# A spectral filter beside an MLP on one core: two-tile width transforms over four PSUM banks, PSUM in zones, leftover rows gathered, the filter chain with fillers in pieces

## The chip, the core and the metric

One core of a Trainium2 chip. TensorE (PE) multiplies matrices from SBUF into PSUM (eight banks), VectorE (DVE), ScalarE (ACT) and GpSimd (POOL) work element by element, SyncE (SP) issues all transfers of this kernel. [...] The metric is the device time of one execution in microseconds (us): 191.66 is the median of three runs of the kernel before (191.43 to 191.84).

## The reference

The input is one sequence of 2048 rows of 640, in bf16. It is normalised by rows, and the output is the input plus two branches of the normalised rows: a filter in the two-dimensional Fourier domain, and an MLP with a GELU.

```python
xn = _layernorm(x, axis=-1)                      # x: (1, 2048, 640)
X  = rfft2(xn.astype(float32)) * (w_r + 1j*w_i)  # w: (2048, 321)
a  = irfft2(X, s=(2048, 640)).astype(bfloat16)
h  = gelu(xn @ w1 + b1)                          # w1: (640, 1536)
return x + a + (h @ w2 + b2)                     # w2: (1536, 640)
```

## The kernel before

The 2048 rows lie on the 128 partitions as 16 tiles of 128 rows by 640 columns. The Fourier transforms are matmuls with constant tables, and a length-2048 transform is split into 128 x 16. The program runs through these steps; the names are those that the rows of the profile show.

1. *Ring*, for each of the 16 tiles `c`: DVE takes the statistics of `XV` (two halves, `stats`), aggregates them (`mv`), adds epsilon (`ve`); POOL raises it to the power -1/2 (`rstd`, one operation for two tiles, L538); DVE makes the shift (`nmr`) and the normalised tile (`T`, L553). PE transposes it with five matmuls against `ident` (L560) into one PSUM bank `tps`, and DVE or ACT copies that to `xnT`, the MLP's operand. DVE also folds the tile about its middle, twice (L572 and L575, into `T` again): 640 columns become four groups of 160. The first transform along the rows, `aps`, multiplies the folded tile by `gtab`: of each group 128 columns as a full matmul, and the 32 left over as a narrow one, 32 columns of output wide, four of them side by side on the partitions of one bank. A copy brings it to `XW` (DVE or ACT).
2. *MLP, first half*: 48 products `hps` of five 128 x 512 matmuls each (`ps<-xnT,W`), each followed by ACT's GELU into `gT` (L598). They need only four finished tiles of `xnT`, so they serve as filler wherever PE would wait.
3. *Filter chain*, for each of 8 pairs of row frequencies. `bps`: the width transform with `etab`, in two halves `v`, each over two banks, both members `n` of the pair beside each other in a bank; per half and member, 128 rows and the 32 left over are multiplied apart (the function `five`). Copies to `Xb`. `cps`: the second part of the row transform with `mtab`, 64 x 64 matmuls, in two halves `r`; copies to `Y`. On DVE the complex product with the filter weights `Wf`: two `T` of 1288 elements (L650), then two `Z` of 644 (L655). `dps`: back with `ntab`, in two halves `hi`, each 8 full matmuls and 8 narrow ones for the leftover 32 rows; copies to `XV`, of which the first use is over.
4. *End*, for each of 8 pairs of tiles: `eps`, the width transform back with `getab` (the same `five`), copies to `Wf` (whose weights are used up), two unfoldings on DVE (L700 and L705), then for each tile `fps`: 24 matmuls of the MLP's second half (`ps<-XW,gT`, with `W2` loaded over `XW`) and 2 with `htab` that add the last part of the row transform. POOL has meanwhile added the bias to the tile of `x` that was loaded once more (`xo<-xr,b2bc`, L713); DVE adds this to `fps` (`ost`, L725), and SP stores it.

The order is not written by hand. The kernel records its operations with their readers, writers, priorities and an estimated duration for each engine that may do it, and a small list scheduler (`Sched.schedule`) walks through simulated time: at each engine it takes, of the operations that could start within 0.03 us of the first, the one of highest priority. PSUM banks and SBUF buffers come out of pools in the same walk (`Pool.find`). `gate` keeps an operation back until others are placed. The result is one fixed list for each engine, in which every instruction waits for its semaphores in order. What is late on the chip is not overtaken: an engine waits at the head of its list. All DMAs are issued by SP, in the order of the program.

Of the kernel before, what the change touches and what calls it, by code (L numbers as in the profile page):

```python
# [13 lines left out]
D = 640  # L14
# [98 lines left out]

class Buf:


    def __init__(self, name, pool=None, size=1):
        self.name, self.pool, self.size = name, pool, size
        self.writers, self.readers = [], []
        self.slot = None  # L120
        self.prev = []
        self.left = None


class Pool:
# [8 lines left out]
    def find(self, size):  # L134
        best = None
        for i in range(0, len(self.free) - size + 1, size):
            if any(self.busy[i:i + size]):
                continue
            t = max(self.free[i:i + size])
            if size == 1 and len(self.free) == 8:  # L140
                t += 0.001 * (not self.busy[i ^ 1])
            if best is None or t < best[0]:
                best = (t, i)
        return best
# [17 lines left out]

LAT = {"pe": 0.2, "dve": 0.12, "act": 0.15, "pool": 0.1}


class Sched:
    def __init__(self, nc, engines):
# [5 lines left out]
    def op(self, engs, prio, emit, reads=(), writes=(), after=(), nbytes=0, gate=()):  # L173
        o = Op()
        o.gate = [g for g in gate if g is not None]
        o.name = writes[0].name if writes else ""
        o.engs = engs
        o.eng = None
        o.prio = prio
        o.emit = emit  # L180
        o.reads, o.writes, o.after = list(reads), list(writes), list(after)
        o.nbytes = nbytes
        o.seq = len(self.ops)
        o.done = False
        o.inc = False
        o.count = None
        o.sem = None
# [8 lines left out]
    def schedule(self):  # L196
# [15 lines left out]
        def avail(o):  # L212
            o.ready = max([0.0] + [d.end for d in o.deps])
# [6 lines left out]
        while left:  # L220
            best = None
            for e in self.engines:
                cands = []
                for o in pend[e]:
# [3 lines left out]
                    ok = True  # L228
                    for b in o.writes:
                        if b.pool is not None and b.slot is None:  # L230
                            f = b.pool.find(b.size)
# [3 lines left out]
                            r = max(r, f[0])  # L235
                    t = max(r, free[e])
                    if ok and len(o.engs) > 1:
                        mine = (t + dict(o.engs)[e], self.engines.index(e))
                        ok = all(e2 == e or (max(r, free[e2]) + d2, self.engines.index(e2)) > mine for e2, d2 in o.engs)
# [27 lines left out]
            for b in o.writes:  # L267
                if b.pool is not None and b.slot is None:
                    b.pool.take(b, b.pool.find(b.size)[1])
# [102 lines left out]
def bass_parallel_sum__spectral_gfnet__dense_activation_gelu__prompt_kernel(  # L372
# [21 lines left out]
    with ExitStack() as es:  # L394
# [32 lines left out]
        Zb = sb("Z", [128, 2, 4 * KP])  # L427
        ost = sb("ost", [128, 3, D])
# [17 lines left out]
        p_xn, p_x1, p_xf, p_xb, p_y, p_t, p_z = Pool(4), Pool(3), Pool(4), Pool(2), Pool(2), Pool(2), Pool(2)  # L446
        p_yo, p_y2, p_yf, p_xr, p_xo, p_os = Pool(3), Pool(2), Pool(3), Pool(4), Pool(3), Pool(3)

        def load(dst, src, buf, nbytes, after=(), reads=()):
            return K.op([("sp", 0.06)], 0, lambda e, _: e.dma_start(dst, src), reads=reads, writes=[buf], after=after, nbytes=nbytes)  # L450
# [8 lines left out]
        def copy(dst, src):  # L459
            def f(e, name):  # L460
                if name == "act":
                    return e.activation(dst(), src(), ACT.Copy)  # L462
# [12 lines left out]
        B_x = [Buf(f"x{g}") for g in range(4)]  # L475
# [4 lines left out]
        def load_x(g):  # L480
            load(view(XV, 4 * g * D, [[1, 4 * D]]), xv[:, 4 * g:4 * g + 4, :].rearrange("p c d -> p (c d)"), B_x[g], 4 * D * 256)
        load_x(0)
        load(ident[:], const["I"], B_id, 32768)
        for j in range(3):
            load(W1[:, :, 512 * j:512 * j + 512], w1v[:, :, 512 * j:512 * j + 512], B_w1s[j], 655360)
            if j == 0:
                load(b1t[:], b1v, B_b1, 3072)
# [273 lines left out]
```

## Time and profile before

| | |
|---|---|
| median of 3 runs | 191.66 us |
| the profiled execution | 190.8 us |
| its span, first to last instruction | 189.2 us |
| PE busy | 163.8 us (87%), 1505 matmuls |
| DVE, ACT, POOL busy | 99.7, 84.5, 28.5 us |
| mean granted clock of TensorE | 0.97 |

The profile is of one execution. Its page gives for each engine the busy share of 40 equal slices of the span in tenths, and the groups of instructions with count and duration; the trace behind it answers with the chain of waits that ended last, timelines of an engine, and sums by window. A timeline's row has the start, the length from the first start to the last end, the engine, the line, the names (`out<-in`) and the count; in brackets stands the idle time before it and what ended that. The names leave out buffer numbers: `ps` is any PSUM bank, `W` is `W1`, `XW` is `XW2`, which later holds `W2`, and `T` holds several of the ring's buffers. `L455` and `L462`/`L463` are helpers that issue all matmuls and all copies, so rows are told apart by their names. Matmuls are pipelined: the busy column of two neighbours overlaps.

### The profile page before, as it was taken

How to read it: one execution, taken by the hardware profiler on the slowest of the kernel's cores; microseconds unless marked ns; L12 is line 12 of the kernel's file. 1: busy time of each engine (PE TensorE's matmuls, PEld its weight loads, DVE VectorE, ACT ScalarE, POOL GpSimd, SP SyncE). 2: the span in 40 equal slices, each digit the busy share in tenths (PEclk: the TensorE clock that was granted, in tenths of full speed). 3: DMA queues.
4: the chain of work that ended last, by engine and by line, in shares of the span. 5: the costliest groups of instructions: out<-in, count | busy, mean ns of one | idle time of the engine just before them, and what ended most of it. 6: DMA issues, size and time to landing. Idle time of an engine off the chain costs nothing.

```text
span 189.2 us, 3594 instructions
## 1 busy us (share of the span) xinstructions
PE 163.8 (87%) x1505; PEld 99.7 (53%) x1505; DVE 99.7 (53%) x248; ACT 84.5 (45%) x123; POOL 28.5 (15%) x32
## 2 busy tenths in 40 slices
PE   0039999996049999999999999999999999998992
PEld 0035555552035454665656576766766676445771
DVE  0998899993055539889191853353524352000311
ACT  2018767755016499999968802020223021661000
POOL 1110111100631000000000013222241225000200
PEclk9999999999658999999999999999999999999998
DMA  6999999999320000000940003232222201000021
GB/s 176 378 388 275 98 110 99 106 96 287 101 83 0 3 0 0 7 3 0 280 139 3 0 13 95 69 107 69 69 71 71 69 35 52 21 0 0 35 69 38
DMA packets 14279, 16.64 MB, mean 88 GB/s; under 512 B 1208, under 2 KB 13496, under 8 KB 14264
## 3 DMA queue, kind: packets, MB, share of 16 engines
q1 hardware_dynamic: 14264, 16.42, 38.9%
q8 instruction: 12, 0.20, 0.5%
q14 instruction: 3, 0.02, 0.1%
HBM read 13.79 MB, written 2.62 MB: 87 GB/s over the span
## 4 chain that ended last, share of the span: by engine, by line
PE 67%; SPq 14%; DMA 10%; DVE 3%; POOL 3%; ACT 1%; issue 1%
PE ps L455 66%; SPq L450 14%; DMA xr<-in_A_x_dram 7%; DMA XV<-in_A_x_dram 2%; POOL xo L713 2%; DVE stats L534 1%; PE ps L560 1%; DVE Y L463 1%; POOL rstd L538 1%; DVE ost L725 0%; ACT XV L462 0%; ACT gT L598 0%; ACT Y L462 0%; DVE T L553 0%; DVE mv L536 0%
## 5 line engine op out<-in xcount | busy, mean ns | idle before, releaser
L455 PE MATMUL ps<-xnT,W 128*128 128x512 bf16 x240 | 57.7, 387 | 0.1
L455 PE MATMUL ps<-XW,gT 128*128 128x320 bf16 x384 | 54.8, 299 | 0.8 <-ACT gT L598 0.8
L455 PEld LDWEIGHTS ps<-XW,gT 128*128 128x128 bf16 x384 | 37.4, 98 | 15.8 <-ACT gT L598 1.5
L598 ACT ACTIVATE gT<-ps,b1col 128x512 bf16<-128x512 f32 x48 | 33.0, 688 | 27.5 <-PE ps L455 27.4
L713 POOL TENSOR_TENSOR xo<-xr,b2bc 128x640 f32<-128x640 bf16 x16 | 22.2, 1393 | 114.7 <-DVE ost L725 101.8
L725 DVE TENSOR_TENSOR ost<-ps,xo 128x640 bf16<-128x640 f32 x16 | 13.2, 824 | 47.2 <-PE ps L455 47.2
L455 PEld LDWEIGHTS ps<-xnT,W 128*128 128x128 bf16 x240 | 22.3, 99 | 24.4 <-issue 1.4
L462 ACT ACTIVATE Wf<-ps 128x640 bf16<-128x640 f32 x15 | 9.9, 703 | 35.5 <-PE ps L455 35.5
L560 PE MATMUL ps<-ident,T 128*128 128x128 bf16 x80 | 7.4, 254 | 13.7 <-DVE T L553 13.7
L534 DVE BATCH_NORM_STATS2 stats<-XV 128x6 f32<-128x320 bf16 x32 | 13.9, 467 | 5.0 <-DMA XV<-in_A_x_dram 5.0
L462 ACT ACTIVATE xnT<-ps 128x640 bf16<-128x640 bf16 x8 | 5.5, 701 | 21.6 <-PE ps L560 21.5
L560 PEld LDWEIGHTS ps<-ident,T 128*128 128x128 bf16 x80 | 6.0, 114 | 15.4 <-DVE T L553 14.6
L455 PE MATMUL ps<-ntab,Z 128*128 128x128 bf16 (+1 forms) x256 | 12.8, 223 | 0.2 <-ACT Y L462 0.2
L650 DVE TENSOR_TENSOR T<-Y,Wf 128x1288 bf16<-128x1288 bf16 x16 | 12.5, 821 | 0.0
L462 ACT ACTIVATE XV<-ps 128x640 bf16<-128x640 f32 x16 | 11.2, 709 | 1.1 <-PE ps L455 0.4
L455 PEld LDWEIGHTS ps<-ntab,Z 128*128 128x128 bf16 (+1 forms) x256 | 9.5, 97 | 3.9 <-issue 0.8
L700 DVE TENSOR_TENSOR Wf<-Wf 128x640 bf16<-128x640 bf16 x16 | 8.0, 537 | 5.8 <-ACT Wf L462 5.8
L455 PE MATMUL ps<-getab,XV 128*128 128x160 bf16 (+1 forms) x128 | 11.0, 234 | 0.0
L455 PE MATMUL ps<-etab,XW 128*128 128x160 bf16 (+1 forms) x128 | 10.9, 234 | 0.1
L538 POOL TENSOR_TENSOR rstd<-ve,mhalf 128x2 f32<-128x2 f32 x8 | 5.8, 722 | 33.8 <-DVE ve L537 33.8
L462 ACT ACTIVATE Xb<-ps 128x640 bf16<-128x640 f32 x13 | 10.5, 911 | 0.5 <-PE ps L455 0.4
L455 PEld LDWEIGHTS ps<-gtab,T 128*128 128x128 bf16 (+1 forms) x128 | 7.0, 101 | 5.7 <-issue 1.1
(35 smaller groups left out, 118.8 us busy)
## 6 DMA issues: line engine op xcount, KB each, us to landing
XV<-in_A_x_dram SPq DMA_DIRECT2D x4, 640.0 KB, 7.9
xr<-in_A_x_dram SPq DMA_DIRECT2D x16, 160.0 KB, 2.2
out_dram<-ost SPq DMA_DIRECT2D x16, 160.0 KB, 1.8
W<-in_B_w_dram SPq DMA_DIRECT2D x3, 640.0 KB, 7.6
XW<-in_B_w_dram SPq DMA_DIRECT2D x1, 1920.0 KB, 8.4
Wf<-in_A_w_r_dram SPq DMA_DIRECT2D x7, 160.5 KB, 14.8
Wf<-in_A_w_i_dram SPq DMA_DIRECT2D x7, 160.5 KB, 15.7
gtab<-c_G SPq DMA_DIRECT2D x1, 512.0 KB, 9.7
```

The lines of the kernel that those rows point to most:

```text
L450: return K.op([("sp", 0.06)], 0, lambda e, _: e.dma_start(dst, src), reads=reads, writes=[buf], after=after, nbytes=nbytes)
L455: ins = e.matmul(o_, lhsT=lw, rhs=rh, start=st, stop=sp_)
L462: return e.activation(dst(), src(), ACT.Copy)
L463: return e.tensor_copy(dst(), src())
L534: K.op([("dve", 0.4)], pr, lambda e, _, c=c, h=h: e.bn_stats(stats[:, c, 6 * h:6 * h + 6], view(XV, c * D + H2 * h, [[1, H2]])), reads=[B_ ...
L538: K.op([("pool", 0.6)], pr, lambda e, _, a=a, b=b: e.tensor_tensor(out=rstd[:, a:b], in0=ve[:, a:b], in1=mhalf[:, a:b], op=ALU.pow), reads ...
L560: ins = e.transpose(ps(tps.slot, 0, 512).bitcast(BF)[:, 128 * j:128 * j + 128], xnv(128 * j, [[1, 128]]), ident[:])
L598: K.op([("act", act_us(512, 1))], pr + 50, lambda e, _, q4=q4, fc=fc, hps=hps: e.activation(gT[:, fc, 512 * q4:512 * q4 + 512], ps(hps.slo ...
L650: t_ops[pair].append(K.op([("dve", dve_us(4 * KP, 2))], pr, lambda e, _, k=k, Y=Y, TB=TB, pair=pair: e.tensor_tensor(out=view(TT, TB.slot ...
L700: K.op([("dve", dve_us(D, 2))], pr + 2, lambda e, _, k=k, op=op, yo=yo, y2=y2: e.tensor_tensor(out=view(Wf, Y2 + y2.slot * 2 * D + (H2 - 1 ...
L713: K.op([("pool", pool_us(640))], 50, lambda e, _, xr=xr, xo=xo: e.tensor_tensor(out=xot[:, xo.slot, :], in0=xrt[:, xr.slot, :], in1=b2bc[: ...
L725: K.op([("dve", dve_us(640))], 95, lambda e, _, xo=xo, os_=os_, fps=fps: e.tensor_tensor(out=ost[:, os_.slot, :].rearrange("p (h n) -> p h ...
```

## The change

Line numbers shift: L538 becomes L554, L455 becomes L467, L462/L463 become L474/L477.

- *Zones and costs.* Each PSUM buffer may have a zone of banks (`ZONE`): `bps` and `eps` the lower four, `hps`, `cps`, `dps` and `fps` the upper four, `tps` and `aps` all. `find` prefers banks that are free in time, in half-used groups. `gate` now also delays an operation to the start of what gates it; priorities stand in a table; the estimates for issuing a DMA rise, and the weights' loads count as slower.
- *Width transforms.* `bps` and `eps` take four banks at once, one for each group `g`, and a pair needs one operation instead of two. The 16 matmuls stay, in another order: four full, eight of 32 rows, four full.
- *Leftover rows in the ring.* The second fold writes the leftover columns of the four groups beside each other (two operations of 256 and 64 elements for one of 320), so that `aps` is five full matmuls instead of four full and four narrow.
- *Leftover rows in the filter.* Four small copies a pair (128 elements each), on DVE, ACT or POOL as the scheduler has it, gather them from `Z` into `Zs`, one of them with the sign turned. `dps` is then ten full matmuls instead of 8 full and 8 narrow.
- *Pieces.* An `hps` is two operations, of three and two matmuls, a `fps` five (four of 6 matmuls, one of 2), each placed by itself.
- *Loads.* `x` comes in eight groups instead of four, in another order among the other loads. The second load of `x`, `xr`, waits in the scheduler until the last `bps` is placed.

```diff
+ZONE = {"hps": [(4, 8)] * 4, "bps": (0, 4), "cps": (4, 8), "dps": (4, 8), "eps": (0, 4), "fps": (4, 8), "tps": (0, 8), "aps": (0, 8)}
...
-            o.ready = max([0.0] + [d.end for d in o.deps])
+            o.ready = max([0.0] + [d.end for d in o.deps] + [d.start for d in o.gate])
...
         load_x(0)
         load(ident[:], const["I"], B_id, 32768)
...
+        load_x(1)
+        load(W1[:, :, 0:512], w1v[:, :, 0:512], B_w1s[0], 655360)
+        load(b1t[:], b1v, B_b1, 3072)
+        load_x(2)
+        load(gtab[:].rearrange("p a b -> p (a b)"), const["G"], B_g, 524288)
+        load_x(3)
...
+                for o_, o0, o1, n in ((128 * k, 0, H2 - 1, 128), (512 + 32 * k, 128, H2 - 129, 32)):
...
-            ring_ops.append(K.op([("pe", 4 * mm_us(128) + 4 * mm_us(32))], pr - 0.2, mms(lambda c=c, xfv=xfv, aps=aps: [
...
+            ring_ops.append(K.op([("pe", 5 * mm_us(128))], pr - 0.2, mms(lambda c=c, xfv=xfv, aps=aps: [
+                (ps(aps.slot + j // 4, 128 * (j % 4), 128 * (j % 4) + 128), xfv(128 * j, [[1, 128]]), gtab[:, c, :], True, True) for j in range(5)]),
...
+            for n, part in ((0, 0), (0, 1), (1, 1), (1, 0)):
+                for g in range(4):
+                    o_ = ps(slot + g, Q4 * n, Q4 * n + Q4)
+                    if part == 0:
+                        lst.append((o_, main(g, n), tab[:, Q4 * g:Q4 * g + Q4], n == 0, n == 1))
+                    else:
+                        lst.append((o_, rem(g, n), tab[32 * g:32 * g + 32, 4 * Q4:5 * Q4], n == 1, n == 0))
...
+            bps = Buf(f"bps{pair}", psum, 4, ZONE["bps"])
...
+        SMALL = [("dve", 0.066 + 128 / 960), ("pool", 0.35), ("act", act_us(128))]
...
+                K.op(SMALL, pr, copy(lambda hi=hi, ZS=ZS: zs(ZS, 256 * hi, [[64, 2], [32, 2], [1, 32]]),
+                                     lambda hi=hi, Z=Z: zk(Z, 2 * KP * hi + 256, [[KP + 1, 2], [1, 2], [2, 32]])), reads=[Z], writes=[ZS])
...
+                    for n, rh in enumerate((NA, NB)):
+                        lst.append((ps(dps.slot + 1, 0, 128), zs(ZS, 256 * hi + 128 * n, [[1, 128]]), rh, n == 0, n == 1))
...
-                K.op([("sp", 0.06)], 0, lambda e, _, c=c, xr=xr: e.dma_start(xrt[:, xr.slot, :], xv[:, c, :]), writes=[xr], nbytes=163840)
+                K.op([("sp", 0.35)], 0, lambda e, _, c=c, xr=xr: e.dma_start(xrt[:, xr.slot, :], xv[:, c, :]), writes=[xr], nbytes=163840, gate=pb_ops)
```

POOL's list, from the first `rstd` on, was:

```order
L538 TENSOR_TENSOR rstd<-ve,mhalf 128x2 x6
L713 TENSOR_TENSOR xo<-xr,b2bc 128x640 x3
L538 TENSOR_TENSOR rstd<-ve,mhalf 128x2 x2
L713 TENSOR_TENSOR xo<-xr,b2bc 128x640 x13
```

And now it is:

```order
L554 TENSOR_TENSOR rstd<-ve,mhalf 128x2 x8
L477 COPY Zs<-Z 128x128
L476 TENSOR_SCALAR Zs<-Z 128x2x64
L477 COPY Zs<-Z 128x128 x6
L477 COPY Zs<-Z 128x2x64
L477 COPY Zs<-Z 128x128
L749 TENSOR_TENSOR xo<-xr,b2bc 128x640 x16
```

The three `xo` have moved from between the `rstd` to behind all of them, and ten gathers of leftover rows stand between.

PE's list in the middle of the filter stage, from one `bps` (`etab`) to the next `hps` (`xnT,W`), was:

```order
L455 MATMUL ps<-etab,XW 128x160 x24
L455 MATMUL ps<-ntab,Z 128x128 x8
L455 MATMUL ps<-ntab,Z 32x128 x8
L455 MATMUL ps<-ntab,Z 128x128 x8
L455 MATMUL ps<-ntab,Z 32x128 x8
L455 MATMUL ps<-Xb,mtab 64x322 x32
L455 MATMUL ps<-ntab,Z 128x128 x8
L455 MATMUL ps<-ntab,Z 32x128 x8
L455 MATMUL ps<-ntab,Z 128x128 x8
L455 MATMUL ps<-ntab,Z 32x128 x8
L455 MATMUL ps<-etab,XW 128x160 x32
L455 MATMUL ps<-xnT,W 128x512 x5
```

Now one pair of six that are alike but for small shifts, from an `etab` to the next:

```order
L467 MATMUL ps<-etab,XW 128x160 x16
L467 MATMUL ps<-Xb,mtab 64x322 x8
L467 MATMUL ps<-ntab,Z 128x128 x8
L467 MATMUL ps<-ntab,Zs 128x128 x2
L467 MATMUL ps<-ntab,Z 128x128 x8
L467 MATMUL ps<-ntab,Zs 128x128 x2
L467 MATMUL ps<-Xb,mtab 64x322 x8
L467 MATMUL ps<-etab,XW 128x160 x16
```

The narrow matmuls are gone, `mtab` is split in two runs, and between the third and the last pairs no `hps` stands any more; 28 of its matmuls stand behind the last `mtab`, between the last `ntab`.

ACT's list at the same place was:

```order
L462 ACTIVATE Y<-ps 128x2x322 x2
L462 ACTIVATE XV<-ps 128x80x8 x2
L462 ACTIVATE Xb<-ps 128x2x2x160 x2
L462 ACTIVATE XV<-ps 128x80x8 x2
L462 ACTIVATE Y<-ps 128x2x322 x3
```

And now, for one pair:

```order
L474 ACTIVATE Xb<-ps 128x2x2x160
L474 ACTIVATE Y<-ps 128x2x322
L474 ACTIVATE XV<-ps 128x80x8 x2
L474 ACTIVATE Y<-ps 128x2x322
L474 ACTIVATE Zs<-Z 128x2x64
```

ACT has all `Y` now (DVE had five of sixteen), 8 of the 16 `Xb` (it had 13), and about one gather a pair; DVE's list has the other eight `Xb` and none of the `Y`.

More of the change, by code (lines that the diff above doesn't have):

```diff
@@ L139, in find @@
             t = max(self.free[i:i + size])
[L140 to L144, printed above, removed]
+            key = (max(t, now), sum(not b for b in self.busy[i & ~1:(i & ~1) + 2]), sum(not b for b in self.busy[i & ~3:(i & ~3) + 4]), t)
+            if best is None or key < best[0]:
+                best = (key, t, i)
+        return best and best[1:]
     def take(self, buf, i):
@@ L160 @@
     pass
+BIAS = {"dve": 0.0}
 LAT = {"pe": 0.2, "dve": 0.12, "act": 0.15, "pool": 0.1}
@@ L725, in bass_parallel_sum__spectral_gfnet__dense_activation_gelu__prompt_kernel @@
+                fin_ops[c] = K.op([("pe", 2 * mm_us(H2))], PRIO["fin"] + 1 - c / 10, mms(lambda c=c, n=n, yf=yf, fps=fps: [
+                    (ps(fps.slot + h, 0, H2), htab[:, c, :], view(Wf, YF + yf.slot * 2 * D + D * n + H2 * h, [[1, H2]]), False, True) for h in range(2)]),
+                    reads=[yf, B_h], writes=[fps], gate=part)
                 K.op([("dve", dve_us(640))], 95, lambda e, _, xo=xo, os_=os_, fps=fps: e.tensor_tensor(
```

198 lines of the change are left out of this document (98 added, 100 removed).

## The prediction

> **What bounds the kernel now.** I read the page first: the span and the busy slices. All times are us.
>
> ```profile
> span 189.2 us, 3594 instructions
> PE   0039999996049999999999999999999999998992
> PEclk9999999999658999999999999999999999999998
> ```
>
> PE is full except at the start, at the end, and in a hole at the tenth slice (each is 4.73 us), behind which its granted clock is 6 and 5 tenths. So TensorE bounds nearly all of it: time falls where PE gets less work, or idles less. The chain that ended last names the hole, and its last row the end of PE's work:
>
> ```profile
> 35.05 14.04 DMA xr<-in_A_x_dram
> ...
> 49.16 4.08 POOL xo L713 x3
> 53.25 0.67 POOL rstd L538
> ...
> 185.91 0.82 DVE ost L725
> ```
>
> Three residual additions (`xo`) stand in POOL's list ahead of the last two `rstd`. They wait for `xr`, which lies behind all loads and lands at 49.09. DVE waits for that `rstd`, and PE for DVE's `T`. PE's timeline shows the price, and what each kind of matmul takes: the difference of two starts, not the busy column, since matmuls overlap.
>
> ```profile
> 28.39 0.56 PE L455 MATMUL ps<-gtab,T 128*128 128x128 bf16 x8
> 28.88 1.25 PE L455 MATMUL ps<-xnT,W 128*128 128x512 bf16 x5
> 29.96 0.56 PE L455 MATMUL ps<-gtab,T 128*128 128x128 bf16 x8
> ...
> 33.70 0.72 PE L560 MATMUL ps<-ident,T 128*128 128x128 bf16 x10
> 34.26 1.24 PE L455 MATMUL ps<-xnT,W 128*128 128x512 bf16 x5
> ...
> 54.64 1.25 PE L560 MATMUL ps<-ident,T 128*128 128x128 bf16 x10 [9.03 <-DVE T L553]
> 55.68 2.34 PE L455 MATMUL ps<-xnT,W 128*128 128x512 bf16 x5
> 57.81 0.86 PE L455 MATMUL ps<-gtab,T 128*128 128x128 bf16 x8
> ...
> 66.06 2.67 PE L455 MATMUL ps<-etab,XW 128*128 128x160 bf16 x32
> 68.57 1.24 PE L455 MATMUL ps<-xnT,W 128*128 128x512 bf16 x5
> ...
> 81.82 1.62 PE L455 MATMUL ps<-ntab,Z 128*128 128x128 bf16 x32
> 83.37 1.35 PE L455 MATMUL ps<-Xb,mtab 64*64 64x322 bf16 x32
> ...
> 103.14 3.92 PE L455 MATMUL ps<-getab,XV 128*128 128x160 bf16 x48
> ...
> 107.97 3.42 PE L455 MATMUL ps<-XW,gT 128*128 128x320 bf16 x24
> 111.23 0.43 PE L455 MATMUL ps<-Wf,htab 128*128 128x320 bf16 x2
> ```
>
> Three stages follow: the ring (norm, transposes, first transform) until the first `etab` at 66.06; the filter stage until the first `getab` at 103.14 (37.08 us, PE without a break); the end stage to the 185.91 above, then 3.3 us of output addition and store. Ten transposes take 0.56 (0.056 each), five 512-column matmuls 1.08 (0.216 each), the 8 `gtab` of a tile 0.49, the 16 `ntab` of a tile 1.55/2 = 0.775, the 32 `etab` of two pairs 2.51, one of the 24 `gT` 3.26/24 = 0.136.
>
> **The change part by part.** *The hole.* POOL's new list has all eight `rstd` ahead of everything that waits for a DMA, and `xr` is issued behind the last `etab`. The 9.03 us go. So does the slow restart: transposes 1.04 instead of 0.56, five matmuls 2.13 instead of 1.08, `gtab` 0.86 instead of 0.56 (busy), together 1.83. What is late next is DVE, whose list is as long as PE's here:
>
> ```profile
> 20.00:30.00 10.00, 10.00 (x80) 5.46 (x79) 9.24 (x33) 7.29 (x11) 0.89 (x2) 1.00 1.24 105
> ```
>
> (The columns: window, PE, PEld, DVE, ACT, POOL busy, clock, DMA.) PE 10.0 and DVE 9.24 of ten: neither can gain alone.
>
> *Ring, PE.* The narrow matmuls (32 output rows) of `aps` go: a tile has 5 full matmuls, 5 x 0.056 = 0.28, for 0.49: 0.21 x 16 = 3.4 less. By count the ring holds 133 instead of 130 `hps` matmuls, 0.6 more. PE: 2.8 less.
>
> *Ring, DVE.* Each second fold is cut in two (256 and 64 elements).
>
> ```profile
> 26.86 0.82 DVE L463 CAST XW<-ps 128x640 bf16<-128x640 f32 x1
> 27.60 0.55 DVE L575 TENSOR_TENSOR T<-T 128x320 bf16<-128x320 bf16 x2
> 28.07 0.55 DVE L572 TENSOR_TENSOR T<-T 128x320 bf16<-128x320 bf16 x2
> ...
> 31.13 0.15 DVE L537 TENSOR_SCALAR ve<-mv 128x2 f32<-128x2 f32 x1
> 31.25 0.21 DVE L536 BATCH_NORM_AGGREGATE mv<-stats 128x2 f32<-128x12 f32 x1
> ...
> 79.52 0.90 DVE L655 TENSOR_TENSOR Z<-T 128x644 bf16<-128x644 bf16 x2
> 80.34 1.56 DVE L650 TENSOR_TENSOR T<-Y,Wf 128x1288 bf16<-128x1288 bf16 x2
> 82.02 0.89 DVE L463 CAST Xb<-ps 128x640 bf16<-128x640 f32 x1
> 82.81 0.87 DVE L655 TENSOR_TENSOR Z<-T 128x644 bf16<-128x644 bf16 x2
> ```
>
> 320 elements step 0.235, 644 step 0.41: 0.54 ns an element, 0.06 fixed. So 256 cost 0.20 and 64 between 0.095 and the 0.12 of a two-element `ve`: 0.29 to 0.32 for 0.235, over 32 pairs 1.8 to 2.7 more. DVE has three `XW` casts where it had six: 3 x 0.74 = 2.2 less (ACT, at 7.29 of ten above, takes them). Sum near zero. The first load is halved, so the first statistics start earlier; a load of 640 KB costs 1.7 at the 388 GB/s of its slice, half of that is 0.8.
>
> ```profile
> GB/s 176 378 388 275 98 110 99 106 96 287 101 83 0 3 0 0 7 3 0 280 139 3 0 13 95 69 107 69 69 71 71 69 35 52 21 0 0 35 69 38
> ```
>
> Ring end: 66.06 - 9.03 - 1.83 - 0.8 = 54.4 if DVE paces it fully, 2.8 less, 51.6, if PE does. I take 53.5, since both were about full. Of the loads that change places the most delayed is the fifth `x` group, 4.2 MB into the queue: some 14 us at the rates above, wanted by DVE's statistics about half way through the ring. No cost.
>
> *Filter stage, PE.* `ntab`: 8 full matmuls, 8 x 0.056 = 0.45, of 0.775; the rest, 0.33, was two groups of four narrow ones with a change of tile shape before and behind. In `gtab` one such group cost 0.49 - 0.22 = 0.27. So a group costs 0.06, four abreast at the price of one, and a change in and out 0.21. After: 10 x 0.056 = 0.56, 0.215 less, x16 = 3.4. `etab`: 160 columns lie between 0.056 (128) and 0.136 (320): 0.069. Half a pair was 4 x 0.069 + 2 x 0.069 + 0.21 = 0.63, which is 2.51/4, so the sum is right. After, a pair is 8 full, two groups of four 32-row matmuls abreast, one change: 8 x 0.069 + 2 x 0.069 + 0.21 = 0.90 instead of 1.255. If only two run abreast, 1.04. That is 0.35 less a pair, 2.8 in the stage. `mtab` stands in 12 runs instead of 5: 7 x 0.21 = 1.5 more; 5 more `hps` matmuls, 1.1. PE's work: 37.1 - 3.4 - 2.8 + 1.5 + 1.1 = 33.5.
>
> *Filter stage, the others.* This is where the saving doesn't come through. `cps`, `dps` and `hps` now share the upper four banks, two double slots, and a pair's `bps` takes all four lower ones. In the middle six pairs PE's list has no `hps` filler at all. All `Y` and `XV` copies are ACT's, the `Xb` half ACT's and half DVE's:
>
> ```profile
> 78.42 1.30 ACT L462 ACTIVATE Y<-ps 128x644 bf16<-128x644 f32 x2
> 79.59 1.32 ACT L462 ACTIVATE XV<-ps 128x640 bf16<-128x640 f32 x2
> 80.77 1.68 ACT L462 ACTIVATE Xb<-ps 128x640 bf16<-128x640 f32 x2
> ...
> 84.10 1.90 ACT L462 ACTIVATE Y<-ps 128x644 bf16<-128x644 f32 x3
> 84.94 1.62 PE L455 MATMUL ps<-ntab,Z 128*128 128x128 bf16 x32 [0.22 <-ACT Y L462]
> 85.86 0.74 ACT L462 ACTIVATE XV<-ps 128x640 bf16<-128x640 f32 x1
> ```
>
> `Y` and `XV` step 0.585, `Xb` about 0.75 (the single `XV` starts 0.15 after the 0.775 of its matmuls). For a pair ACT has 0.75 + 4 x 0.585 + one `Zs`. No row shows `Zs` (128 elements, SBUF to SBUF): between 0.12 (a fifth of 0.585) and 0.585; I take 0.25, nearer the small one. Sum 3.35. Then a bubble: the second `dps` goes to the slot that the first `Y` empties. From that `Y`'s start it is 0.84 to the matmul (84.94 against 84.10), 0.56 of matmuls, 0.15 to the copy, 1.55 in all; ACT has 2 x 0.585 = 1.17 to do. 0.38 are lost: 3.75 a pair (3.73 before rounding). PE's list is in order: behind the waiting `dps` stand the next `mtab` and `etab`, for which ACT's next `Y` and both engines' `Xb` wait. DVE has 0.79 (`Xb`, 82.02 to 82.81) + 1.48 (two `T`, 1.56 less the overlap that `Z` shows) + 0.82 + 2 `Zs` of about 0.2 = 3.5, PE 0.90 + 2 x 0.45 + 1.12 = 2.9, idle for 0.85. Over the stage ACT has 16 `Y`, 16 `XV`, 8 `Xb`, 10 `Zs`, 9 gelu (512 elements, taken like a `Y`): 18.7 + 6 + 2.5 + 5.3 = 32.5; with 2.7 of bubbles (7 pairs) and some 3.5 before its first `Y` and behind its last `XV`: 39. Bounds: 3.25 a pair without a bubble, some 36; and 4.6, what a pair takes now (37.08/8), some 45.5.
>
> [...]
>
> POOL's `Zs`, one or two a pair, have no row either: an `xo` of 640 elements takes 4.08/3 = 1.36, a fifth of it is 0.27. They run between a pair's `Z` and its `dps`, two thirds of a pair later; hidden, unless they take three times as long.
>
> *End stage.* PE alone. `getab` gains 0.35 x 8 = 2.8; 62 instead of 70 `hps` matmuls, 1.7. 82.7 becomes 78.2. `fin` in quarters has the same matmuls. Their cover: copying a pair's `eps` (about 1.1) lies under 12 `gT` matmuls (1.63). `W2`'s load, now ahead of `xr` in SP's queue, is issued at the last `etab`, 13 us of matmuls before its first use:
>
> ```profile
> XW<-in_B_w_dram SPq DMA_DIRECT2D x1, 1920.0 KB, 8.4
> ```
>
> It lands in time with 4 us to spare; if it did not, `fin` waits for it and 1 to 2 are lost. The first `xr` behind it is wanted only by the first output addition, 5 us into the stage.
>
> *Sum.* 53.5 + 39 + 78.2 + 3.3 = 174.0 span; 189.2 was 190.8 as executed, so 175.6; the median of the runs is 191.66, 0.9 above that execution: **176.5**. By stages: -12.6, +1.9, -4.5.
>
> **The rivals.** *ACT's bubble vanishes* (its rows at 78.42 to 80.77 are back to back, which speaks for it): stage 36, 173.5. *Two double slots are too few*: a bubble at both `dps` and before `Xb` bring a pair back to 4.6: stage 45.5, 183. For: 84.10 shows PE and ACT waiting for each other with more banks. Against: the bubbles would have to be 1.25 a pair. *The clock falls in the filter stage*, the one that ends slower. PE idles a quarter of each pair there, in gaps of up to 0.5. The restart rows show what a low clock costs: 1.83 more on 2.2 (0.56 + 1.08 + 0.56). Of the delay of 33.5 us of work the first 5.5 vanish in idle time (39 - 33.5); the 15.2 gained are gone once 25 us of the work run slow (25 x 0.83 = 5.5 + 15.2); all of it gives 61 instead of 39, 198.5. Against: the clock was 1.00 in the window above, and fell by the slices only with the gap of 9.03. [...] *The change doesn't do what it says*: four row groups don't run abreast; 0.14 x 16 = 2.2, half of it hidden, 177.6.
>
> **How the numbers follow.** Forecast (with the unabreast case) 0.70, its own range 173.5 to 180; bubble gone 0.13; too few slots 0.12; clock 0.05, of which 0.01 in part (15 us slow: 15 x 0.83 - 5.5 = +7, 183.5), 0.01 at the crossing and 0.03 beyond it. The range takes in the first three with half a microsecond or two for a ring end between 51.6 and 55.2: 171.5 to 184. Differences within 0.2% are what runs of this kernel can't tell apart; only that crossing lies there, 0.01. Faster 0.70 + 0.13 + 0.12 + 0.01 = 0.96, slower 0.03.
>
> **What would show it.** Right: no PE wait over 2 us between 14 and the end; the first `etab` near 53.5 and the first `getab` near 92.5; `etab` 0.90 a pair, `ntab` 0.56; PE at 7 to 8 tenths and ACT at 9 in the middle of the filter stage; end stage 78. Wrong: PE full throughout the filter stage, a clock under 0.9 there, a wait for `Wf` or `W2`, or a ring end after 56.

## The result and the profile after

The changed kernel takes 176.25 us (median of 4 runs, 175.82 to 177.15), the kernel before 191.75 on the same chip (4 runs, 191.43 to 192.44): a ratio of 0.919, 95% interval 0.915 to 0.924. The profiled execution took 177.15, 0.9 above the median; the other three had spans of 173.8 to 174.4.

From the page of the changed kernel: the span, PE's busy slices (4.38 us each) and its clock.

```profile
span 175.1 us, 3375 instructions
PE   0046999999999997887899999999999999998992
PEclk9999999999999999999999999999999999999999
```

The hole of the tenth slice is gone, and the granted clock is at 9 tenths or more in every slice, 1.00 on average. New is a dip to 7 and 8 in slices 16 to 20, in the filter stage. PE's timeline of the changed kernel at the ends of the stages, with DVE's last output addition:

```profile
9.11 0.19 PE L534 MATMUL ps<-ident,b1t 12*128 12x12 bf16 x1 [9.11 <-DMA b1t<-in_B_b_dram]
10.11 1.25 PE L576 MATMUL ps<-ident,T 128*128 128x128 bf16 x10 [0.81 <-DVE T L569]
...
54.95 1.07 PE L467 MATMUL ps<-etab,XW 128*128 128x160 bf16 x16
55.86 1.24 PE L467 MATMUL ps<-xnT,W 128*128 128x512 bf16 x5
...
93.57 1.07 PE L467 MATMUL ps<-getab,XV 128*128 128x160 bf16 x16
...
172.03 0.82 DVE L761 TENSOR_TENSOR ost<-ps,xo 128x640 bf16<-128x640 f32 x1 [2.71 <-PE ps L467]
```

The ring ends at 54.95, the filter stage takes 38.62, the end stage 78.46 to the last output addition, and 3.1 are left: 11.1 less, 1.5 more and 4.3 less than before. The 16 `etab` of a pair step 0.91 (54.95 to 55.86). In the kernel before, the first two rows were:

```profile
7.19 0.19 PE L518 MATMUL ps<-ident,b1t 12*128 12x12 bf16 x1 [7.19 <-DMA b1t<-in_B_b_dram]
9.25 1.25 PE L560 MATMUL ps<-ident,T 128*128 128x128 bf16 x10 [1.88 <-DVE T L553]
```

The first transposes come later now, not earlier, and behind a later `b1t`. DVE's list in the changed kernel shows the link: the copy `b1col` waits for PE's matmul on `b1t`, and the first `nmr` stands behind it.

```profile
9.34 0.17 DVE L536 COPY b1col<-ps 128x12 f32<-128x12 f32 x1 [1.25 <-PE ps L534]
9.42 0.15 DVE L556 SCALAR_TENSOR_TENSOR nmr<-mv,rstd 128x2 f32<-128x2 f32 x1
```

The middle of the filter stage, from its windows (columns as in the prediction) and from the timelines of PE and ACT over one pair:

```profile
60.00:70.00 10.00, 8.98 (x136) 5.48 (x135) 8.43 (x14) 9.52 (x18) 1.32 (x4) 1.00 0.01 2
70.00:80.00 10.00, 8.90 (x152) 5.45 (x145) 9.62 (x21) 9.45 (x17) 1.05 (x3) 1.00 0.01 2
```

```profile
73.36 0.62 PE L467 MATMUL ps<-ntab,Z 128*128 128x128 bf16 x8 [0.49 <-ACT Y L474]
73.82 0.28 PE L467 MATMUL ps<-ntab,Zs 128*128 128x128 bf16 x2
74.03 0.47 PE L467 MATMUL ps<-Xb,mtab 64*64 64x322 bf16 x8
74.43 1.08 PE L467 MATMUL ps<-etab,XW 128*128 128x160 bf16 x16
75.44 0.47 PE L467 MATMUL ps<-Xb,mtab 64*64 64x322 bf16 x8
75.84 0.62 PE L467 MATMUL ps<-ntab,Z 128*128 128x128 bf16 x8
76.30 0.28 PE L467 MATMUL ps<-ntab,Zs 128*128 128x128 bf16 x2
77.06 0.62 PE L467 MATMUL ps<-ntab,Z 128*128 128x128 bf16 x8 [0.48 <-ACT Y L474]
```

```profile
74.14 0.70 ACT L474 ACTIVATE XV<-ps 128x640 bf16<-128x640 f32 x1 [0.23 <-PE ps L467]
74.73 0.70 ACT L474 ACTIVATE Y<-ps 128x644 bf16<-128x644 f32 x1
75.32 0.32 ACT L474 ACTIVATE Zs<-Z 128x128 bf16<-128x128 bf16 x1
75.55 0.91 ACT L474 ACTIVATE Xb<-ps 128x640 bf16<-128x640 f32 x1
76.31 0.69 ACT L474 ACTIVATE Y<-ps 128x644 bf16<-128x644 f32 x1
76.89 0.72 ACT L474 ACTIVATE XV<-ps 128x640 bf16<-128x640 f32 x1
77.83 0.70 ACT L474 ACTIVATE XV<-ps 128x640 bf16<-128x640 f32 x1 [0.23 <-PE ps L467]
```

A pair takes 3.70 (73.36 to 77.06). Below, a middle pair is one of this pattern, and there are fewer of them than the six named ahead of the prediction: from `etab` to `etab` the steps are 2.51, 3.02, 3.60, 3.02, 3.63, 3.70 and 3.70, and from the last `etab` to the first `getab` it is another 15.44. In a middle pair PE waits half a microsecond for the first `Y` before its second `ntab` tile, ACT a quarter for that tile before its second `XV` (0.94 from `XV` to `XV` for 0.58), as predicted. A run of 8 `mtab` steps 0.40. Whether ACT's list sets the 3.70, as the prediction had it, these rows don't tell; the experiments do.

### The profile page after: what moved, and what is told of

Same layout as the page of the kernel before. It is cut to its first block, busy times and chain, and to the rows that moved or that the text cites. A ratio compares the mean times of both kernels' runs of the same rounds, so it can differ in the third digit from the quotient of the medians.

```text
span 175.1 us, 3375 instructions
## 1 busy us (share of the span) xinstructions
PE 154.2 (88%) x1350; PEld 95.2 (54%) x1361; DVE 109.6 (63%) x296; ACT 82.1 (47%) x129; POOL 32.5 (19%) x42
## 4 chain that ended last, share of the span: by engine, by line
PE 77%; ACT 12%; DMA 4%; DVE 3%; issue 1%; SPq 1%
PE ps L467 74%; DMA b1t<-in_B_b_dram 4%; ACT Xb L474 3%; ACT XV L474 3%; PE ps L576 3%; ACT Y L474 3%; ACT gT L616 1%; SPq L462 1%; ACT L616 1%; DVE T L592 1%; DVE T L569 1%; ACT Zs L474 1%; DVE T L588 1%; DVE ost L761 0%; DVE stats L550 0%
## 5 line engine op out<-in xcount | busy, mean ns | idle before, releaser
L467 PE MATMUL ps<-xnT,W 128*128 128x512 bf16 x229 | 57.3, 387 | 1.9 <-ACT xnT L474 0.8
L467 PE MATMUL ps<-XW,gT 128*128 128x320 bf16 x384 | 55.4, 299 | 0.8 <-ACT gT L616 0.8
L467 PEld LDWEIGHTS ps<-XW,gT 128*128 128x128 bf16 x384 | 37.2, 98 | 16.1 <-ACT gT L616 1.9
L467 PEld LDWEIGHTS ps<-xnT,W 128*128 128x128 bf16 x240 | 22.1, 99 | 24.3 <-ACT gT L616 2.6
L474 ACT ACTIVATE Wf<-ps 128x640 bf16<-128x640 f32 x8 | 5.6, 704 | 37.3 <-PE ps L467 37.3
L554 POOL TENSOR_TENSOR rstd<-ve,mhalf 128x2 f32<-128x2 f32 x8 | 5.7, 707 | 42.9 <-DVE ve L553 42.9
L474 ACT ACTIVATE XV<-ps 128x640 bf16<-128x640 f32 x16 | 11.1, 707 | 2.5 <-PE ps L467 2.5
L467 PE MATMUL ps<-ntab,Z 128*128 128x128 bf16 x128 | 9.8, 220 | 1.8 <-ACT Y L474 1.8
L474 ACT ACTIVATE XW<-ps 128x640 bf16<-128x640 f32 x13 | 9.1, 702 | 4.7 <-PE ps L467 4.4
L592 DVE TENSOR_TENSOR T<-T 128x256 bf16<-128x256 bf16 x64 | 11.2, 233 | 0.0
L474 ACT ACTIVATE xnT<-ps 128x640 bf16<-128x640 bf16 x8 | 5.6, 701 | 11.5 <-PE ps L576 11.5
L474 ACT ACTIVATE Y<-ps 128x644 bf16<-128x644 f32 x16 | 10.9, 706 | 0.1
L477 DVE CAST Wf<-ps 128x640 bf16<-128x640 f32 x8 | 6.6, 823 | 6.8 <-PE ps L467 6.4
L736 DVE TENSOR_TENSOR Wf<-Wf 128x640 bf16<-128x640 bf16 x16 | 10.1, 673 | 0.4
L467 PEld LDWEIGHTS ps<-ntab,Z 128*128 128x128 bf16 x128 | 7.6, 98 | 4.9 <-ACT Y L474 2.6
L477 POOL COPY Zs<-Z 128x128 bf16<-128x128 bf16 x9 | 3.4, 383 | 34.5 <-DVE Z L676 34.5
L477 DVE CAST Xb<-ps 128x640 bf16<-128x640 f32 x8 | 7.1, 883 | 4.3 <-PE ps L467 4.3
```

The source lines that it names most:

```text
L467: ins = e.matmul(o_, lhsT=lw, rhs=rh, start=st, stop=sp_)
L474: return e.activation(dst(), src(), ACT.Copy, scale=scale)
L477: return e.tensor_copy(dst(), src())
L554: K.op([("pool", 0.6)], pr, lambda e, _, a=a, b=b: e.tensor_tensor(out=rstd[:, a:b], in0=ve[:, a:b], in1=mhalf[:, a:b], op=ALU.pow), reads ...
L592: K.op([("dve", dve_us(2 * n, 2))], pr - 0.2, lambda e, _, op=op, x1v=x1v, xfv=xfv, o_=o_, o0=o0, o1=o1, n=n: e.tensor_tensor(out=xfv(o_, ...
L736: K.op([("dve", dve_us(D, 2))], pr + 2, lambda e, _, k=k, op=op, yo=yo, y2=y2: e.tensor_tensor(out=view(Wf, Y2 + y2.slot * 2 * D + (H2 - 1 ...
```

## The experiments

All kernels at a glance, by their traces: start of the first `etab`, length of the filter stage, length of the end stage to the end of the last matmul, and the step of a middle pair (mean of the last two steps from `etab` to `etab`); then the median of the runs (the last two have one run). From xr_late_alone on, each four rows ran on one chip.

| kernel | first `etab` | filter | end | pair | time | ratio to before |
|---|---|---|---|---|---|---|
| before | 66.06 | 37.07 | 82.74 | | 191.75 | |
| changed | 54.95 | 38.62 | 78.43 | 3.70 | 176.25 | 0.919 (0.915 to 0.924) |
| xr_late_alone | 55.89 | 38.89 | 82.74 | | 182.93 | 0.953 (0.945 to 0.961) |
| b1_first | 53.66 | 38.61 | 78.43 | 3.70 | 176.54 | 0.918 (0.913 to 0.922) |
| xr_not_gated | 60.02 | 38.60 | 78.43 | 3.70 | 181.64 | 0.944 (0.937 to 0.950) |
| etab_in_halves | 55.16 | 41.34 | 81.06 | 4.04 | 182.12 | 0.945 (0.938 to 0.952) |
| first_dps_narrow | 53.88 | 39.34 | 78.42 | 3.70 | 177.06 | 0.920 (0.914 to 0.925) |
| second_dps_narrow | 53.68 | 39.41 | 78.42 | 3.81 | 177.26 | 0.921 (0.915 to 0.927) |
| no_gather_copies | 54.30 | 38.32 | 78.49 | 3.70 | 176.44 | 0.916 (0.911 to 0.921) |
| gathering_undone | 54.20 | 40.04 | 78.43 | 3.81 | 177.63 | 0.923 (0.917 to 0.928) |
| after_again | 54.37 | 38.61 | 78.43 | 3.70 | 176.61 | 0.924 (0.919 to 0.929) |
| b1_first_again | 53.54 | 38.62 | 78.43 | 3.70 | 176.01 | 0.920 (0.916 to 0.925) |
| ring_pe_dearer | 56.10 | 38.60 | 78.42 | 3.70 | 178.29 | |
| ring_dve_cheaper | 53.33 | 38.60 | 78.50 | 3.70 | 175.78 | |

The stages repeat to a few hundredths where a kernel doesn't touch them (from b1_first on, 38.60 to 38.62 for the filter stage and 78.42 to 78.50 for the end stage), so a difference of 0.1 in one can be read, while the times of so close kernels overlap.

**xr_late_alone.** Of the change, the hole alone, in the kernel before:

```diff
-                K.op([("sp", 0.06)], 0, lambda e, _, c=c, xr=xr: e.dma_start(xrt[:, xr.slot, :], xv[:, c, :]), writes=[xr], nbytes=163840)
+                K.op([("sp", 0.06)], 0, lambda e, _, c=c, xr=xr: e.dma_start(xrt[:, xr.slot, :], xv[:, c, :]), writes=[xr], nbytes=163840, gate=pb_ops)
```

> The kernel before with one edit: the loads of xr are planned behind the last etab. PE, DVE and ACT keep their lists; on POOL the three xo move behind the last two rstd. The prediction's theory: the 9.03 hole and the 1.83 of slow restart go and nothing takes their place, so the first etab comes at 66.06 - 10.9 = 55.2, the other stages stay at 37.1 and 82.7, and the time is 191.75 - 10.9 = 180.9. Then of the 15.5 that the whole change gained, two thirds are this one line. Rival: DVE had a backlog that the hole let it work off, and the hole comes back in small waits: 183 or more, first etab at 57 or later.

The ring ends 10.2 earlier, at 55.89, so the hole is this one line. But the span falls by 8.3 (189.2 to 180.9), 2.5 short of the expected 10.9. PE reaches the transposes behind which the hole lay at 46.30, 0.7 later than the 45.61 at which it stopped before (54.64 - 9.03). This lateness is there from the start: the first transposes come at 9.35 instead of 9.25, and the first five 512-column matmuls (16.81, before 16.70) take 2.31 instead of 1.68; why, no run says. Without it the line would be worth about the 10.9 foreseen in the ring. And 1.8 are given back in the filter stage, where `xr` now lands. PE at both places, then DVE and POOL in the filter stage:

```profile
46.30 0.72 PE L560 MATMUL ps<-ident,T 128*128 128x128 bf16 x10
...
92.13 1.63 PE L455 MATMUL ps<-ntab,Z 128*128 128x128 bf16 x32 [1.76 <-DVE Z L655]
```

```profile
87.23 0.89 DVE L655 TENSOR_TENSOR Z<-T 128x644 bf16<-128x644 bf16 x2
...
88.90 3.17 DVE L655 TENSOR_TENSOR Z<-T 128x644 bf16<-128x644 bf16 x2
```

```profile
88.33 5.00 POOL L713 TENSOR_TENSOR xo<-xr,b2bc 128x640 f32<-128x640 bf16 x3 [39.45 <-DMA xr<-in_A_x_dram]
```

Two `Z` take 0.89 alone and 3.17 beside POOL's `xo`, and PE waits 1.76 for them. An `xo` doesn't only hold up what stands behind it on POOL: each `Z` beside it takes about as long as an `xo` does (3.17/2 = 1.59, 5.00/3 = 1.67).

**b1_first.** The load of `b1t` goes from its place behind the first part of `W1` to the place right behind `ident`:

```diff
         load(ident[:], const["I"], B_id, 32768)
+        load(b1t[:], b1v, B_b1, 3072)
         load_x(1)
         load(W1[:, :, 0:512], w1v[:, :, 0:512], B_w1s[0], 655360)
-        load(b1t[:], b1v, B_b1, 3072)
```

> The changed kernel with the load of b1t put right behind ident's. In the changed kernel b1t lands at 9.07, and the copy b1col stands in DVE's list ahead of the first nmr, so that the first transposes wait until 10.11; the prediction had them at 8.45. If this is what made the first etab come 1.45 later than predicted, the first transposes start near 8.6, the first etab moves from 54.95 to 53.5, and the time is 1.0 to 1.5 lower (175.0). Rival: the ring is paced by its loads or by the full lists of PE and DVE further on, the early start is eaten there, and the time stays within 0.3 of the changed kernel's.

PE's timeline:

```profile
4.09 0.17 PE L534 MATMUL ps<-ident,b1t 12*128 12x12 bf16 x1 [4.09 <-DMA b1t<-in_B_b_dram]
8.81 1.25 PE L576 MATMUL ps<-ident,T 128*128 128x128 bf16 x10 [4.55 <-DVE T L569]
```

The first transposes start 1.30 earlier, and the whole 1.29 arrives at the first `etab`. The late `b1t` is what the profiled execution of the changed kernel had too much. The times of the two, from different chips, don't show it, and `b1t`'s landing moves: in the kernels of the table that load it in the changed kernel's place PE's first matmul starts between 7.7 (second_dps_narrow) and 9.11 (changed), and the first `etab` for the most part follows. So the two were run again side by side.

**after_again, b1_first_again.**

> The changed kernel once more, beside the next one on the same chip: b1t's landing has moved between 7.7 and 9.1 in the kernels that load it in the changed kernel's place, and the first etab with it, between 53.7 and 55.2. The same is expected here, and a span of 173.8 to 175.2.

> The changed kernel with b1t loaded behind ident, again. Theory: b1t is no longer late, so the first etab is at 53.7 whatever the loads do, and the span is 0 to 1.3 below the changed kernel's, 0.5 on average. Rival: no difference that the times can show.

176.61 (176.24 to 177.26, 6 runs) against 176.01 (175.72 to 176.28, 6 runs): 0.6 less, 0.3%, with ranges that just touch; the spans of the profiled executions are 174.5 and 173.7. So the kernel with `b1t` first is ahead of the changed kernel, by little.

**xr_not_gated.** The one line taken out of the changed kernel:

```diff
-                K.op([("sp", 0.35)], 0, lambda e, _, c=c, xr=xr: e.dma_start(xrt[:, xr.slot, :], xv[:, c, :]), writes=[xr], nbytes=163840, gate=pb_ops)
+                K.op([("sp", 0.35)], 0, lambda e, _, c=c, xr=xr: e.dma_start(xrt[:, xr.slot, :], xv[:, c, :]), writes=[xr], nbytes=163840)
```

> The changed kernel with the same one line taken out again. The planner's new costs of a load keep all eight rstd ahead on POOL all the same; what moves is three xo ahead of the first Zs on POOL, and the seven xr ahead of W2 in SP's queue. Theory: both are hidden (xr lands long before the first Zs at about 62, and W2 has some 13 us to land), so the time is the same within 0.5 and PE shows no hole in the ring. Rival: the hole comes back, 187; or W2 lands late behind xr and fin waits 1 to 2.

My theory fell: the ring ends 5.1 later. All `rstd` are ahead on POOL as expected, and no hole of the old kind comes back. DVE, POOL, and PE:

```profile
49.96 1.92 DVE L569 TENSOR_SCALAR T<-XV,rstd,nmr 128x640 bf16<-128x640 bf16 x2
51.80 2.94 DVE L588 TENSOR_TENSOR T<-T 128x320 bf16<-128x320 bf16 x2
...
55.67 0.55 DVE L588 TENSOR_TENSOR T<-T 128x320 bf16<-128x320 bf16 x2
```

```profile
50.30 4.25 POOL L749 TENSOR_TENSOR xo<-xr,b2bc 128x640 f32<-128x640 bf16 x3 [0.57 <-DMA xr<-in_A_x_dram]
```

```profile
55.80 0.72 PE L467 MATMUL ps<-gtab,T 128*128 128x128 bf16 x5 [2.34 <-DVE T L592]
56.31 2.34 PE L467 MATMUL ps<-xnT,W 128*128 128x512 bf16 x5
```

Two folds take 0.55, and 2.94 while POOL adds: one `xo` each (4.25/3 = 1.42). The two `T` ahead of them (L569), which read one tile and two columns, are held too: 1.92, for 0.75 shortly before (46.09). It is what xr_late_alone showed (3.17 for 0.89), on work for which PE waits. The transfers don't explain it: the DMA share is 0.18 from 50 to 60, and in the changed kernel 1.24 from 20 to 30, where two folds take 0.55 (25.02). Why DVE is held beside `xo`, no run shows. The granted clock is 0.83 from 50 to 60, for 1.00 in the four windows of ten ahead of that, and behind the wait of 2.34 five 512-column matmuls show 2.34 instead of 1.24. Of the 5.1, PE's two waits for DVE are 3.3 (0.97 and 2.34), and the slow matmuls behind them about 1.5.

**etab_in_halves.** Each half of the pair with its own groups of narrow matmuls, in the same banks:

```diff
-            for n, part in ((0, 0), (0, 1), (1, 1), (1, 0)):
-                for g in range(4):
+            for v in range(2):
+              for n, part in ((0, 0), (0, 1), (1, 1), (1, 0)):
+                for g in (2 * v, 2 * v + 1):
...
```

> The changed kernel, every list the same, but the 16 etab of a pair and the 16 getab of a pair are given in two halves as before: two groups of two 32-row matmuls twice, instead of two groups of four. A pair should cost 1.25 instead of 0.91. Theory (PE has slack in the filter stage and none behind it): the filter stage stays within 0.7 of 38.6, since only the pairs at its ends are PE's, the end stage grows by 8 x 0.34 = 2.7, and the time is 2.7 to 3.4 higher. Rival: PE paces the filter stage too, and the time is 5.4 higher. Other rival: the four row groups were no gain over two, 0 to 1.

The rival holds: 2.7 in the filter stage and 2.6 in the end stage. PE idles in every middle pair, and yet 0.34 more of its work costs the pair all of 0.34. ACT, at the corresponding place:

```profile
77.56 0.32 ACT L474 ACTIVATE Zs<-Z 128x128 bf16<-128x128 bf16 x1
78.13 0.91 ACT L474 ACTIVATE Xb<-ps 128x640 bf16<-128x640 f32 x1 [0.25 <-PE ps L467]
```

Now `Xb` waits for `etab`. Back in the changed kernel's rows, two ways lead from the second `ntab` tile (73.36) to the `Xb` copy (75.55). By PE: 0.67 to `mtab`, 0.40 to `etab`, 1.12 from its start to `Xb`. By ACT: 0.78 to `XV`, 0.59 to `Y`, 0.59 to `Zs`, 0.23 to `Xb`. Both make 2.19, as any two chains of starts between the same two rows must; which of them has room shows where the same work stands elsewhere. Where ACT's next copy is ready, it starts 0.20 after a `Zs` (66.52 and 82.72), not 0.23. So ACT stands still for some 0.03 here, too little to be shown as idle time, and PE's way is the longer by a hair. From `Xb`, 0.76 to `Y` and 0.75 to the next second `ntab` close the loop: 3.70. This near tie is why ACT looks as if its list were the limit. The next four kernels try this.

**first_dps_narrow, second_dps_narrow.** One `ntab` tile of the pair takes its leftover rows as before (with hi == 0, or with hi == 1):

```diff
+                    if hi == 0:
+                        for n in range(2):
+                            for g, k0 in enumerate((0, 1, 1, 2)):
+                                r, rh = (((0, NA), (1, NN)) if g < 2 else ((1, NA), (0, NB)))[n]
+                                lst.append((ps(dps.slot + 1, 0, 128)[32 * g:32 * g + 32], z(r, k0 + 256, 32), rh, n == 0, n == 1))
+                        return lst
                     for n, rh in enumerate((NA, NB)):
```

> The changed kernel, all lists the same and all Zs copies still made, but the first ntab tile of each pair takes its leftover rows as before, in two groups of four narrow matmuls: 0.22 more on PE, eight times 1.7. In a middle pair PE runs the first tile, then waits 0.49 for a Y, then runs the second. Theory after the first runs (two loops of nearly one length set the pair: ACT's copies, and second ntab, mtab, etab, Xb, Y, second ntab): the first tile lies on neither, so the middle pairs stay at 3.70 and only pairs at the ends pay, 0.3 to 0.9 in all. Rival (PE's work paces the stage): 1.7.

> The same for the second ntab tile of each pair, again 1.7 more on PE. Theory: the second tile lies on both loops, a middle pair goes from 3.70 to 3.92, and the stage is 1.5 to 1.9 longer. If only ACT's own work set the pair, without the wait of its second XV for the second tile: 0.3 to 0.9, as with the first tile. If PE's work paced the stage: 1.7 here too, so it is the pair of runs that tells.

The first tile costs a middle pair nothing and the stage 0.72; PE's wait shrinks instead, from 0.49 to 0.37:

```profile
76.20 0.62 PE L467 MATMUL ps<-ntab,Z 128*128 128x128 bf16 x8 [0.37 <-ACT Y L474]
```

The second does cost a middle pair, but 0.11, not 0.22, and the stage 0.79, half of what was expected. PE's rows:

```profile
72.08 0.85 PE L467 MATMUL ps<-ntab,Z 128*128 128x128 bf16 x16 [0.49 <-ACT Y L474]
72.86 0.47 PE L467 MATMUL ps<-Xb,mtab 64*64 64x322 bf16 x8
```

From this tile to `mtab` it is 0.78 instead of 0.67: 0.11. My estimate: of the 0.21 that the prediction worked out for the change into a narrow group and out of it, `mtab`, in tiles of 64 x 64, needs the one half anyway, so that the group adds one change there, not two. No run tried that by itself; the changed kernel's rows agree with it: 16 `etab` step 0.91 ahead of 512-column matmuls (54.95 to 55.86) and 1.01 ahead of `mtab` (74.43 to 75.44), so that the way into `mtab` costs 0.10 without a narrow group, too. PE's work alone does not pace the middle; the place of the work in the loop decides.

**no_gather_copies, gathering_undone.** The first keeps the wide matmuls, on a zeroed `Zs`, so that the leftover rows are missing from its result; the second has the narrow ones for both tiles. In both the copies are taken out of the lists once these are made:

```diff
         K.schedule()
+        zs_ops = [o for o in K.ops if o.name.startswith("ZS")]
+        K.ops = [o for o in K.ops if o not in zs_ops]
+        for o in K.ops:
+            o.deps = [d for d in o.deps if d not in zs_ops]
+        for e in K.engines:
+            K.order[e] = [o for o in K.order[e] if o not in zs_ops]
```

> The changed kernel without any of the 32 Zs copies: the ntab matmuls read a Zs that is zeroed once, so the leftover rows of the result are left out. PE's list is the same; ACT loses 10 copies (a step of 0.23 each), DVE 12, POOL 10. Theory (two loops): ACT's loop of a middle pair falls from 3.70 to 3.47, but that of PE stays at 3.64 (second ntab to the end of etab 1.98, 0.15 to the Xb copy, 0.76 to the Y behind it, 0.75 to the next second ntab), so the pair gains 0.06 and the stage 0.3 to 0.8. The prediction's view (ACT's list with its bubble alone sets the pair): 0.23 a pair and more at the ends, 1.6 to 2.4.

> The changed kernel with the gathering alone undone: no Zs copies, narrow matmuls for both tiles as before, all else the same. PE has 3.4 more. Theory (two loops): the loop of PE grows to 3.64 + 0.22 = 3.86, ACT's is 3.47 + 0.22, so a middle pair goes from 3.70 to 3.86 and the pairs at the ends pay 0.43 each; in all 1.5 to 2.5. The prediction's view (ACT alone): -0.23 + 0.22 in the middle, so 0.5 to 1.0 from the ends. Rival (PE's work): 3.4.

Without the copies the pair stays at 3.70 and the stage gains 0.30. ACT in a middle pair:

```profile
73.97 0.70 ACT L474 ACTIVATE Y<-ps 128x644 bf16<-128x644 f32 x1
74.79 0.91 ACT L474 ACTIVATE Xb<-ps 128x640 bf16<-128x640 f32 x1
```

From `Y` to `Xb` it is 0.82 without `Zs`, exactly the 0.59 + 0.23 with it: ACT waits for `etab` as long as the copy would take. The prediction's view, 0.23 a pair, is refuted. With the narrow matmuls back for both tiles the pair is 3.81 and the stage 1.42 longer, just below the lower end of the two loops' expectation (1.5) and over the upper end of ACT's (1.0). So the gathering, priced at 3.4 on PE, is worth 1.4. Most of it falls behind the last `etab`: from there to the first `getab` it is 16.41 instead of 15.44, and the last `ntab` tiles stand between 512-column matmuls there, without a wait of PE.

**ring_pe_dearer, ring_dve_cheaper.** On top of b1_first, the five matmuls of `aps` as four wide and four narrow; and, apart from that, the 32 small folds left out (by the same lines as the `Zs`; the leftover rows that they would make are zero).

```diff
-                (ps(aps.slot + j // 4, 128 * (j % 4), 128 * (j % 4) + 128), xfv(128 * j, [[1, 128]]), gtab[:, c, :], True, True) for j in range(5)]),
+                (ps(aps.slot, 128 * j, 128 * j + 128), xfv(128 * j, [[1, 128]]), gtab[:, c, :], True, True) for j in range(4)] + [
+                (ps(aps.slot + 1, 0, 128)[32 * g:32 * g + 32], xfv(512 + 32 * g, [[1, 32]]), gtab[:, c, :], True, True) for g in range(4)]),
```

> The kernel of b1_first with the narrow matmuls of before in aps (four of 128 rows and four of 32 instead of five of 128), lists and folds the same: 0.21 a tile, 3.4 more on PE in the ring. If PE paces the ring, the first etab comes 3 to 3.4 later than 53.66; if DVE does, 0 to 0.5 later. The prediction put the ring between the two: 1.5 to 2.5.

> The kernel of b1_first without the 32 small folds (64 elements each, a step of 0.10): the rows gathered there are zeroed once and left out of the result. DVE has 3.2 less in the ring, PE's list is the same. If DVE paces the ring, the first etab comes 2.5 to 3.2 earlier than 53.66; if PE does, 0 to 0.5 earlier. The prediction's view, both about full: 0.5 to 1.5.

Two windows of ring_dve_cheaper:

```profile
20.00:30.00 10.00, 10.00 (x73) 5.45 (x73) 6.93 (x25) 7.49 (x12) 0.71 (x1) 1.00 1.24 97
...
40.00:50.00 10.00, 10.00 (x78) 5.55 (x77) 9.08 (x36) 8.16 (x14) 1.41 (x2) 1.00 1.04 152
```

PE is at 10.0 with DVE at 6.9 and 9.1; in b1_first DVE was at 7.5 and 9.8 in the same windows, and PE at 10.0 too. The first `etab` comes 2.4 to 2.6 later (56.10 against 53.54 and 53.66) with 3.4 more on PE, and 0.2 to 0.3 earlier with 3.2 less on DVE. The first transposes didn't start together, though: at 8.34 with the dearer PE and at 9.07 with the cheaper DVE, against 8.60 and 8.81, and in b1_first such a shift arrived whole at the first `etab`. Counted from the first transposes, the ring is 2.8 to 2.9 longer with 3.4 more on PE, and 0.6 to 0.7 shorter with 3.2 less on DVE. PE paces the ring, most of the way.

## Why the prediction was right, point by point

The forecast was 176.5 with a span of 174.0, by way of 53.5, 39 and 78.2. By stages the profiled execution has 54.95, 38.62 and 78.46. That is 1.1 more in the span: the ring is 1.45 over, the rest together 0.3 under. In the filter stage the size is right, but not the reason.

- **The hole.** Right in place and nearly in size: 9.03 + 1.83 = 10.9 foreseen, 10.2 found with that line alone, where the ring's start was 0.7 late for another reason. What is late next was named as DVE; it was PE.
- **The early start, 0.8, was the step that failed.** In the profiled execution the first transposes came 0.86 later (10.11 against 9.25), not 0.8 earlier. The estimate looked at the halved first load alone; but `b1t` stands later in the queue, lands at 9.11 instead of 7.19, and `b1col`, which waits for it, stands in DVE's list ahead of the first `nmr`. The prediction costed the loads that change places, and passed over the smallest. With `b1t` first the start is 0.44 earlier than before, half the 0.8: the first statistics begin 1.15 earlier (3.83 for 4.98), but DVE's list has a statistic of the second load ahead of the first `ve`, and waits 0.52 there. The ring then ends at 53.54 to 53.66, beside the forecast of 53.5.
- **The ring's lists.** 53.5 was taken between DVE's pace (54.4) and PE's (51.6), because both were about full. They were not alike: counted from the first transposes, PE's work counts for about 0.85 of its size there (2.8 to 2.9 of 3.4), DVE's for a fifth (0.6 to 0.7 of 3.2). For PE alone the prediction had 51.6, or 52.0 with the start that came; that 53.5 fits so well is in part luck, and no run tried where the other 1.6 goes.
- **PE's sizes.** Right: `etab` 0.91 for 0.90, where 1.04 was the price with two row groups abreast, so that this rival is out; 0.40 in a run of 8 `mtab`. The extra runs of `mtab`, priced at 0.21 each, were not tried; the rows show the 0.10 of the way in.
- **The filter stage: right number, wrong owner.** ACT's list with its bubble was to give 3.75 a pair and 39; it is 3.70 and 38.6. But the loop runs through PE as well, and by PE it is just as long. That the sum fits is in part luck: the bubble was counted for seven pairs, and ACT idles before an `XV` in this way only four times (0.23 each, at 74.14, 77.83, 81.54 and 84.46); the rest of what ACT loses lies at the two ends of the stage. So "This is where the saving doesn't come through" was wrong: the shorter `etab` was called idle PE's time, and is worth 2.7 in this stage, as etab_in_halves shows. Of the gathering only 1.4 of the 3.4 reckoned arrive. The rival in which row groups are not abreast had "half of it hidden"; none of that in `etab` would have been.
- **`Zs` on ACT.** Taken 0.25; from start to start it is 0.20 where ACT's next copy is ready, and 0.23 in the middle pairs, where it costs nothing. The row shows 0.32 as the copy's length; the next copy starts before that is over.
- **The end stage.** 78.46 for 78.2, PE alone: the shorter `getab` again, 2.6 by etab_in_halves, and the fewer `hps`.
- **The rivals.** The bubble did not vanish: 0.36 on ACT in a middle pair for the 0.38 foreseen (0.94 less 0.58). Two double slots were not too few: 3.70 a pair, not 4.6. The clock stood at 1.00 through the filter stage with PE waiting 0.49 in each middle pair, so pauses of this length didn't bring it down here; in xr_not_gated, with a wait of 2.34, it did fall (0.83 from 50 to 60).

Open is what the zones and the loss of fillers cost by themselves: the stage is 1.5 longer than before although PE has less to do there, and no kernel undid the zones alone.

## What to carry to other kernels

An engine that idles in every round is not free: follow one round from start to start through all engines, and add up each way between two meeting points, since work on the longest way costs its full length however idle its engine looks (here 0.34 more of `etab` cost 0.34 a pair, with PE waiting 0.49 in it). A load of 3 KB is worth its place in the queue when a copy that waits for it stands ahead of the first urgent work in an engine's list (here 1.29 at the first `etab` of the profiled executions, 0.6 in the medians side by side). And what GpSimd adds in SBUF belongs where VectorE has nothing urgent of the kinds that were held here: additions of two tiles in SBUF (2.94 for 0.55, and 3.17 for 0.89), and the scaling of one (1.92 for 0.75).

## What the runs showed that was not expected

- POOL's additions hold up DVE: beside `xo`, two 320-element folds took 2.94 instead of 0.55, and two 644-element `Z` 3.17 instead of 0.89. The change needs its late `xr` for this as much as for POOL's order: without it the ring ends 5.1 later though no `rstd` is held up.
- A narrow group costs 0.11 in front of `mtab` (0.78 for 0.67), half of the 0.22 that the prediction had from a group between wide matmuls.
- The landing of the 3 KB `b1t`, behind 640 KB of `W1` in one queue, moved between 7.7 and 9.1 from kernel to kernel with the same loads ahead of it, and most of the differences between the ring ends of those kernels follow it.
